# Queries asked for before keys and values, half of the first weights asked for later, and outer sums ahead of other work, at the seam of a two-part kernel

## The chip, the cores and the metric

The kernel runs on one core of one Trainium2 chip. The metric is the device time of one execution in microseconds (us), measured from outside the profile; lower is better. A profile is a separate execution, recorded by the hardware; its span, from the first to the last instruction, is a little shorter than the time of the same execution.

Engines are named as in the profile: PE is TensorE's matmuls and PEld its weight loads, DVE is VectorE, ACT ScalarE, POOL GpSimd. SP is SyncE, which here only issues DMA transfers. [...]

## The reference

Two blocks follow each other: a recurrent attention without softmax (a decaying state per head), and a feed-forward layer with a leaky ReLU.

```python
batch, n_heads, seq, head_dim = (4, 8, 768, 64)
for t in range(S):
    state = gamma[None, :, None, None] * state + np.einsum('bhd,bhe->bhde', k[:, :, t], v[:, :, t])
    y[:, :, t] = scale * np.einsum('bhd,bhde->bhe', q[:, :, t], state)
...
n_tokens, d_model, d_ff = (3072, 512, 2048)
h = x @ w_in
g = np.maximum(0.01 * h, h)
return (g @ w_out).astype(np.float32)
```

The 3072 tokens are 4 batches of 768, and the 512 columns of x are 8 heads of 64. q, k and v are float32; the weights come as float64 and are turned into float32 in the kernel.

## The kernel before, in words

**Tiles and stages.** The sequence is cut into six chunks c = 0 to 5 of 128 tokens (C = 128). A chunk of all four batches is 512 tokens, kept as two halves of N = 256. For a chunk, the attention makes x, and the feed-forward layer takes x through four units u = 0 to 3 of 512 hidden columns each. Each unit has a hidden product (x by w_in) and an output product (the activations g by w_out), added up over the units.

The attention of a chunk goes by batches b, from chunk 2 on by pairs of them. Scores are queries times keys (`scores_of_pair`, L369), sums for the state are keys times values (L380). DVE masks the scores (`am`, L387) and adds the sums to the states. Then `joint_visit` multiplies values with scores and states with queries (L444, L427) and DVE writes x (L466). POOL scales the values with the decay ahead of this (`decay_v`, L161).

Products of the feed-forward layer use seven products of half-size blocks in place of eight (Strassen's scheme in Winograd's form), with sums of blocks on DVE: `differences` makes sums of x or g, `add_sums` and `sum_of_unit` sums of weights. In the function `seven` (matmuls at L662) the products M1 to M7 of one unit are made one after another, as a generator: each step of it is one product of eight matmuls, followed by the ACT or DVE work that takes it from its PSUM bank.

**Two parts, and the seam.** In the first part (chunks 0 and 1, up to some 230 us) the float64 weights are loaded in 32 raw pieces and turned into float32 by ACT and DVE (`powers`, `begin_mantissas`, `end_mantissas`); each piece's buffer is free when DVE's instruction at L595 has read it. From the finished units more sums of weights are made and written to a DRAM buffer `kept` (`keep_unit`, L1031). In the second part (chunks 2 to 5, N2 = 16 steps n, one for each chunk and unit) the hidden product uses the scheme on two levels: `inner` (matmuls at L1182) makes seven products for each of seven outer blocks, which are split into group 0 (four blocks) and group 1 (three). `outer` adds the results of a unit up on DVE, and its leaky ReLU runs on ACT (`leaky`, L1218). The weights for `inner` are streamed from `kept`: `load_unit(n, 0)` loads `wa` (L1058, L1059) and `load_unit(n, 1)` loads `wb` (L1062, L1063). The output products stay with `seven`.

The seam is where the parts meet: the last units of chunk 1, the attention of chunk 2 and the beginning of chunk 3, and the first `inner`. What the change touches lies there.

**What sets the order.** Nothing is planned by a program: each engine gets its instructions in the order in which the code writes them. In the first part, dictionaries (`hidden_more`, `output_more`) name functions to be called after step s of a generator: `s3=[...]` means after the fourth product. In the second part the steps are drawn with `products(steps, n)`. So the order on SP is the order of calls too, and a load whose buffer is still in use holds back the loads behind it.

- When the last raw piece, n = 31, is done, `end_mantissas` asks for chunk 2's first pair: values and keys with `of_pair(2, 0, 1)` and `of_pair(2, 0, 0)` (L136), then two batches of queries and keys in another layout with `load_qk` (L119; both called queries below). These lie in buffers of the tags `qk` and `kv`, two of each, which the raw pieces 28 to 31 used before: pieces 28 and 30 those of `qk`, 29 and 31 those of `kv`.
- `begin_units` (after M1 of the output product of chunk 0, unit 3) asks for `wa` and `wb` of step 0. The buffer of `wb` is that of unit 6 of the weights, parts of which are still to be written to `kept`.
- `next_heads` (after M4 of the same product) asks for chunk 3's first pair: values, keys, then queries with `ahead`, and gives POOL the decay of the values.
- After the first part, `last`, the output product of chunk 1 and unit 3, is drawn in pieces: four products, the scores of chunk 3's first pair, M7, `inner(0, 0)`, `outer(0, 0)`, M3, `inner(0, 1)`, M4, the first product of `inner` of step 1 (`begun`), and then `outer(0, 1)`. The loop over n follows, whose first pass draws the other products of `begun`.

Of the kernel before, what the change touches and what calls it, by code (L numbers as in the profile page):

```python
# [22 lines left out]
def kernel(  # L23
# [50 lines left out]
    def new_pair(h):  # L74

        pairs = units.setdefault(N_UNITS - 1, [])
        if len(pairs) == h:
            pairs.append(work.tile([128, 2, 2, 256], FP32, tag="raw", bufs=3, name=f"last{h}"))
# [39 lines left out]
    def load_qk(c, b, queue=nc.sync):  # L118
        queue.dma_start(out=heads[c, b][0], in_=qk[c, b])  # L119
# [9 lines left out]
    def of_pair(c, b, kind, place=None):  # L129

        if place is None:
            place = work.tile([128, 2, H, D], FP32, tag="kv", bufs=AHEAD,
                              name=f"{'kv'[kind]}_{c}_{b}")
        for n in range(2):
            (keys, vals)[kind][c, b + n] = place[:, n]
        nc.sync.dma_start(out=place, in_=kv[c, b + kind])  # L136
# [69 lines left out]
    def new_o(c, name="o"):  # L206
        return work.tile([128, 4, 2, N], FP32, tag=f"o{int(c > 0)}", name=f"{name}_{c}")
# [106 lines left out]
    def ahead(c, b):  # L314

        if c >= NC:
            return
        if b < 2:
            x = work.tile([128, 2, HP, C], FP32, tag="qk", bufs=AHEAD, name=f"qk_{c}_{b}")
        else:  # L320
            if b == 2:
                room[c] = new_o(0).rearrange("p i k n -> p (i k n)")
            x = room[c][:, ds((b - 2) * 2 * HP * C, 2 * HP * C)]
            x = x.rearrange("p (s a t) -> p s a t", s=2, a=HP)
        heads[c, b] = [x]
        load_qk(c, b)
# [149 lines left out]
    def pair_of_banks(name):  # L476

        ps = two_banks(name).rearrange("p j a t -> p j (a t)")
        return [ps[:, j] for j in range(2)]
# [7 lines left out]
    def early_visit(c, b):  # L487
        def do():
            joint_visit(c, b, [pair_of_banks(f"yp{n}_{c}_{b}") for n in range(2)])
        return do  # L490
# [27 lines left out]
    def load_piece(n, place=None):  # L518
        if n >= N_PIECES:
            return  # L520
        if not f64:
            nc.sync.dma_start(out=piece(n), in_=weights[n].rearrange("p (h n) -> p h n", h=2))
            return
        if place is None:
            tag, bufs = ("raw", 3) if n < N_PIECES - 4 else (("qk", "kv")[n % 2], AHEAD)
            raws[n] = work.tile([128, W], I64, tag=tag, bufs=bufs, name=f"raw{n}")
        else:
            raws[n] = place.bitcast(I64)
        nc.sync.dma_start(out=raws[n], in_=weights[n])
# [13 lines left out]
    def end_mantissas():  # L543
        n = done["mantissas"]
        done["mantissas"] += 1
        mantissas_ended(n)
        if n != 3:
            load_piece(n + 4 if n < 3 else n + 3)
        if n == N_PIECES - 1:
            new_pair(2)  # L550
            for b in range(2):
                heads[2, b] = [work.tile([128, 2, HP, C], FP32, tag="qk", bufs=AHEAD,
                                         name=f"qk_2_{b}")]
            of_pair(2, 0, 1)
            of_pair(2, 0, 0)
            for b in range(2):
                load_qk(2, b)
        if n % 4 == 3 and n > 7:
            add_sums(n // 4)

# [37 lines left out]
    def mantissas_ended(n):  # L598
        if f64:
            z, f = zs.pop(n), piece(n)  # L600
            raws.pop(n)
            nc.vector.scalar_tensor_tensor(out=f, in0=f, scalar=2.0 ** -20, in1=z.bitcast(BF16),
                                           op0=ALU.mult, op1=ALU.mult)
# [7 lines left out]
    def add_sums(k, last=True):  # L611

        a11, a21, a12, a22, s1, s2, s4 = (block(k, i) for i in range(7))
        plus(s1, a21, a22)
        minus(s2, s1, a11)
        minus(s4, a12, s2)
        if last:
            last_sum(k)
# [194 lines left out]
    def differ(c):  # L813
        def do():
            if xs[c][1] is None:
                xs[c][1] = new_t(c, f"t_{c}")
            differences(*xs[c])
        return do
# [96 lines left out]
    steps = direct(0, 0, x, parts[0][1], 0)  # L915
# [44 lines left out]
    steps = direct(0, 0, x, parts[0][1], 1)  # L960
# [20 lines left out]
    later = hidden(1, 0, x1, t1, *parts[1][1:], order=FIRST)  # L981
# [66 lines left out]
    def at_of(n):  # L1048
        return 2 + n // NU, n % NU

    def load_unit(n, group):

        if n >= N2:
            return
        u = at_of(n)[1]
        if group == 0:
            wa = streamed[0]
            nc.sync.dma_start(out=wa[:, :, 0:1], in_=kept[u][:, :, 0:1])  # L1058
            nc.sync.dma_start(out=wa[:, :, 1:4], in_=kept[u][:, :, 3:6])  # L1059
        else:  # L1060
            wb = streamed[1]
            nc.sync.dma_start(out=wb[:, :, 0:2], in_=kept[u][:, :, 1:3])  # L1062
            nc.sync.dma_start(out=wb[:, :, 2:3], in_=kept[u][:, :, 6:7])  # L1063

    def begin_units():

        streamed.append(work.tile([128, 7, 4, C], FP32, tag="late4", name="wa"))
        load_unit(0, 0)
        flat = work.tile([128, 28 * C], FP32, tag="late6", name="wb")
        streamed.append(flat[:, 0 : 21 * C].rearrange("p (j i n) -> p j i n", j=7, i=3))  # L1070
        load_unit(0, 1)

    def next_heads():
        of_pair(3, 0, 1)
        of_pair(3, 0, 0)
        for b in range(2):
            ahead(3, b)
        for b in range(2):
            decay_v(3, b)

# [10 lines left out]
                     s3=[keep_unit(3)], s4=[early_visit(2, 2)],  # L1091
# [7 lines left out]
        (1, 2): dict(s0=[sum_of_unit(2, 3)], s1=[keep_unit(2)]),  # L1099
        (0, 3): dict(s0=[begin_units, early_scores(2, 0, spare(0))],  # L1100
                     s1=[lambda: differences(*parts[1][1:])],
                     s3=[early_visit(2, 0), differ(2), next_heads],
                     s6=[sums(2, 0)]),
    }

# [63 lines left out]
    def inner(n, group, held=False):  # L1169

        products(inner_steps(n, group, held), 8)
# [33 lines left out]
    m1, m4, m5, u2 = (made_of[0][:, :, i] for i in range(4))  # L1205
    m7, m2, m3 = (made_of[1][:, :, i] for i in range(3))

    def outer(n, group):

        if group == 0:  # L1210
            gs[n] = new_g(*at_of(n))
        g = gs[n][1]

        def to(i):
            return g[:, i].rearrange("p k (h n) -> p (k h) n", h=2)

        def leaky(i):
            nc.scalar.activation(g[:, i], g[:, i], AF.Prelu, alpha=0.01)  # L1218

        if group == 0:  # L1220
            plus(u2, u2, m1)
            plus(to(1), u2, m5)
            return
        plus(to(0), m1, m2)
        leaky(0)
        plus(to(1), to(1), m3)
        leaky(1)
        plus(u2, u2, m7)
        plus(to(3), u2, m5)
        leaky(3)  # L1230
        plus(to(2), u2, m4)
        leaky(2)

    def products(steps, n):

        for _ in range(n):
            next(steps, None)
# [22 lines left out]
    outer(0, 0)  # L1260
    products(last, 1)
    inner(0, 1)
    products(last, 1)
    begun = inner_steps(1, 0, held=True)
    products(begun, 1)
    outer(0, 1)

    for n in range(N2):
        c, u = at_of(n)
        more = n + 1 < N2  # L1270
        if u == 0:
            os[c] = new_o(c)
        visiting = c + 1 < NC and u < 2
        if n + 1 < N2:
            differences(*gs[n][1:])
        if n + 1 < N2 and u == NU - 1:
            sums_of_x(c + 1, 1)
        if n + 1 < N2:
            if n == 0:
                products(begun, 7)  # L1280
            else:
                inner(n + 1, 0, held=visiting)
            outer(n + 1, 0)
        if visiting and u == 0:
            xs[c + 1] = new_x(c + 1)
        if visiting:
            joint_visit(c + 1, 2 * u)
        steps = output(c, os[c], [gs.pop(n)], u == 0, u == NU - 1, room=room if more else last_room,
                       order=FUSED if more else LAST)
        products(steps, 3)  # L1290
        if c + 1 < NC and u < 2 and following(c + 1, 2 * u):
            scores_of_pair(*following(c + 1, 2 * u))
        if visiting:
            load_unit(n + 2, 0)
        products(steps, 1)
        if c + 1 < NC and u == 1:
            differences(*xs[c + 1])
        if c + 1 < NC and u == 2:
            sums_of_x(c + 1, 0)
        if more:  # L1300
            inner(n + 1, 1)
            for i in range(2) if visiting else ():
                ahead(c + 2, 2 * u + i)
            products(steps, 1)
            outer(n + 1, 1)
        if n + 2 == N2:
            differences(*gs[n + 1][1:])
        products(steps, 3)
# [92 lines left out]
```

## Time and profile before

| what | value |
|---|---|
| time, three runs | 642.95, 643.23, 644.82 us; median 643.23 |
| time of the profiled execution | 643.72 us |
| span of the profile | 641.8 us |
| PE busy | 632.5 us, 99% of the span |
| DVE busy | 462.5 us, 72% |
| ACT busy | 269.0 us, 42% |
| POOL busy | 22.6 us, 4% |
| bytes moved by DMA | 113.42 MB |

The page of the profile gives busy times by engine, and the span in forty slices of 16 us. Its chain of waits is followed back from the last instruction to what released each; PE has 90% of it and DMA 3%. A busy PE is not a PE at its full rate: matmuls overlap, and the clock that the chip grants PE can be lower. That clock is given in tenths for each slice. A "wait" is idle time of an engine just before an instruction, with the event that ended it. In rows of a timeline, `x32` is the number of like instructions merged into the row; names are the program's, such as `qk` for queries.

### The profile page before, as it was taken

The page shows a single profiled execution, that of the slowest core. Times are in us where ns is not written, and L with a number is a line of the kernel's source. Part 1 is how long each engine was busy: PE and PEld are TensorE (multiplying, and loading weights), DVE is VectorE, ACT ScalarE, POOL GpSimd, SP SyncE. Part 2 cuts the span into 40 slices and gives each one's busy share as a digit, 9 for nine tenths or more (in the row PEclk, how much of TensorE's full clock was granted, in tenths as well). Part 3 has the DMA queues.
Part 4 walks back from the last instruction along what each step waited for, and adds up shares of the span by engine and source line. Part 5 has one row for each costly group of instructions (what it writes and reads, how often), then busy time and mean ns, then how long its engine had stood idle before and what let it go on. Part 6 is the DMA issues. An engine that isn't in the chain of part 4 may idle for free.

```text
span 641.8 us, 14287 instructions
## 1 busy us (share of the span) xinstructions
PE 632.5 (99%) x6086; PEld 570.6 (89%) x6086; DVE 462.5 (72%) x760; ACT 269.0 (42%) x515; POOL 22.6 (4%) x45
## 2 busy tenths in 40 slices
PE   8999999999999989999999999999999999999997
PEld 5888888888888879899999998999999999999996
DVE  5679769889979956657776756778737778637655
ACT  4876557257252114352342443523424423533521
POOL 2000000000011010101000001000010000000000
PEclk9999999999999989999999999999999999999999
DMA  8931327455962988284844582854445336545201
GB/s 332 406 122 44 121 66 241 131 196 163 304 226 100 358 299 269 90 284 144 271 121 141 160 257 82 295 170 152 148 152 193 92 117 193 160 153 164 86 1 67
DMA packets 87536, 113.42 MB, mean 177 GB/s; under 512 B 3240, under 2 KB 71720, under 8 KB 87472
## 3 DMA queue, kind: packets, MB, share of 16 engines
q1 hardware_dynamic: 87168, 111.88, 52.6%
q8 instruction: 48, 0.79, 0.5%
q10 hardware_dynamic: 304, 0.62, 0.3%
q14 instruction: 16, 0.13, 0.1%
HBM read 93.35 MB, written 19.14 MB: 175 GB/s over the span
## 4 chain that ended last, share of the span: by engine, by line
PE 90%; DMA 3%; DVE 3%; ACT 1%; issue 1%; SPq 0%; DVEq 0%
PE bank L662 31%; PE bank L1182 27%; PE C_o L662 4%; PE B_o L662 4%; PE A_o L662 4%; PE A_h L662 3%; PE C_h L662 3%; PE B_h L662 3%; DMA qk<-in_qk_dram 2%; PE D_o L662 2%; PE d L683 2%; PE D_h L662 2%; PE bank L444 1%; PE bank L380 1%; PE bank L369 1%; PE bank L427 1%
## 5 line engine op out<-in xcount | busy, mean ns | idle before, releaser
L606 DVE TENSOR_TENSOR o<-o,bank 128x512 f32<-128x512 f32 (+2 forms) x91 | 58.6, 661 | 55.0 <-PE bank L662 33.5
L606 DVE TENSOR_TENSOR made<-made,bank 128x512 f32<-128x512 f32 (+1 forms) x96 | 56.4, 618 | 57.0 <-PE bank L1182 52.6
L662 PE MATMUL bank<-g,w 128*128 128x256 f32 x384 | 89.9, 382 | 0.0
L662 PEld LDWEIGHTS bank<-g,w 128*128 128x128 f32 x384 | 70.7, 190 | 9.2
L1182 PEld LDWEIGHTS bank<-x,wb 128*128 128x128 f32 x672 | 77.6, 192 | 0.8
L1182 PE MATMUL bank<-x,wb 128*128 128x128 f32 x672 | 77.6, 275 | 0.0
L1182 PE MATMUL bank<-x,wa 128*128 128x128 f32 x512 | 68.8, 276 | 0.6 <-ACT made L1188 0.6
L662 PE MATMUL bank<-gd,w 128*128 128x256 f32 x288 | 66.1, 379 | 0.0
L1182 PEld LDWEIGHTS bank<-x,wa 128*128 128x128 f32 x512 | 63.8, 192 | 2.4 <-ACT bank L1186 0.8
L662 PEld LDWEIGHTS bank<-gd,w 128*128 128x128 f32 x288 | 54.7, 190 | 7.4
L1182 PE MATMUL bank<-t,wa 128*128 128x128 f32 x384 | 53.3, 275 | 0.0
L1218 ACT ACTIVATE g<-g 128x512 f32<-128x512 f32 x64 | 39.4, 631 | 31.5 <-DVE g L606 31.5
L1182 PEld LDWEIGHTS bank<-t,wa 128*128 128x128 f32 x384 | 48.0, 192 | 0.0
L1186 ACT COPY bank<-bank 128x512 f32<-128x512 f32 (+1 forms) x32 | 16.7, 522 | 67.8 <-PE bank L1182 67.5
L606 DVE TENSOR_TENSOR g<-made 128x512 f32<-128x512 f32 x64 | 42.7, 688 | 1.1
L755 ACT COPY bank<-bank 128x512 f32<-128x512 f32 x17 | 9.7, 570 | 71.7 <-PE bank L662 71.6
L609 DVE TENSOR_TENSOR gd<-g,gd 128x512 f32<-128x512 f32 x48 | 33.2, 692 | 4.9
L773 ACT COPY bank<-bank 128x512 f32<-128x512 f32 x16 | 9.1, 570 | 49.9 <-PE bank L662 49.9
L662 PE MATMUL bank<-g,last 128*128 128x256 f32 x120 | 29.1, 388 | 0.0
L662 PE MATMUL bank<-gd,last 128*128 128x256 f32 (+1 forms) x124 | 27.5, 373 | 0.0
L662 PE MATMUL A_h<-x,w 128*128 128x256 f32 x112 | 26.6, 380 | 0.0
L662 PEld LDWEIGHTS bank<-gd,last 128*128 128x128 f32 x124 | 22.8, 190 | 3.2 <-DVE gd L609 0.3
(223 smaller groups left out, 1030.6 us busy)
## 6 DMA issues: line engine op xcount, KB each, us to landing
wa<-kept SPq DMA_DIRECT2D x16, 1344.0 KB, 7.7
raw<-in_weights_dram SPq DMA_DIRECT2D x31, 512.0 KB, 4.4
wb<-kept SPq DMA_DIRECT2D x16, 896.0 KB, 5.4
wa<-kept SPq DMA_DIRECT2D x16, 448.0 KB, 4.4
wb<-kept SPq DMA_DIRECT2D x16, 448.0 KB, 6.2
out_dram<-o SPq DMA_DIRECT2D x23, 256.0 KB, 3.4
kept<-w SPq DMA_DIRECT2D x12, 448.0 KB, 5.7
qk<-in_qk_dram SPq DMA_DIRECT2D x10, 512.0 KB, 7.9
```

The costliest lines, as they stand in the source:

```text
L369: nc.tensor.matmul(at[j][ts(h, 64), n, m, i], lhsT=x[ts(j, 64), 1, a, ts(h, 64)], rhs=x[ts(j, 64), 0, a, ts(h, 64)], start=(n == 0 and a = ...
L380: nc.tensor.matmul(sums[h][ts(j, 64), n, a], lhsT=key[ts(h, 64), 2 * a + j], rhs=val[ts(h, 64), 2 * a + j], start=(n == 0 and a == 0), sto ...
L427: mm = nc.tensor.matmul(at[n][j][ts(i, 64), m, ts(h, 64)], lhsT=by_half[h][ts(j, 64), n, a], rhs=x[ts(j, 64), 0, a, ts(h, 64)], start=(n = ...
L606: nc.vector.tensor_tensor(out=out, in0=a, in1=b, op=ALU.add)
L609: nc.vector.tensor_tensor(out=out, in0=a, in1=b, op=ALU.subtract)
L662: nc.tensor.matmul(to, lhsT=block(w, sa)[:, k, ts(i, 128)], rhs=rhs[:, k, a:z], start=(first and (i == 0 or split) and n == 0 and k == 0), ...
L683: nc.tensor.matmul(banks[r][:, i, :], lhsT=block(2 * u, r + 2 * kh)[:, k, ts(i, 128)], rhs=x[:, 2 * kh + th, k, :], start=(step == 0 and i ...
L755: nc.scalar.copy(out=bank_of("B"), in_=ps)
L773: nc.scalar.copy(out=bank_of("D"), in_=ps)
L1182: nc.tensor.matmul(ps[q][:, i], lhsT=w[:, j, i], rhs=part_of(moving[i], s), start=(i == 0 and m in ("M1", "M5", "M4")), stop=True, skip_gr ...
L1186: nc.scalar.copy(out=ps[3], in_=ps[0])
L1218: nc.scalar.activation(g[:, i], g[:, i], AF.Prelu, alpha=0.01)
```

## The change

It has three parts, and the computation stays as it was.

1. The queries are asked for ahead of values and keys, for chunk 2's first pair in `end_mantissas` and for chunk 3's in `next_heads`. Values are still asked for before keys.
2. The load of `wb` for step 0 is taken from `begin_units` and comes after `next_heads`, three products later.
3. `outer(0, 1)` is called before M4 of `last` and not after the first product of `begun`. It puts its five DVE sums into the queue at once, but collects its four leaky ReLUs in a list. Two of them come after the first product of `begun`, the other two after its third. The loop's first pass then draws five products of `begun` in place of seven.

```diff
@@ end_mantissas
+            load_qk(2, 0)
+            load_qk(2, 1)
             of_pair(2, 0, 1)
             of_pair(2, 0, 0)
-            for b in range(2):
-                load_qk(2, b)
@@ begin_units
         load_unit(0, 0)
         flat = work.tile([128, 28 * C], FP32, tag="late6", name="wb")
         streamed.append(flat[:, 0 : 21 * C].rearrange("p (j i n) -> p j i n", j=7, i=3))
-        load_unit(0, 1)
 
     def next_heads():
+        for b in range(2):
+            ahead(3, b)
         of_pair(3, 0, 1)
         of_pair(3, 0, 0)
-        for b in range(2):
-            ahead(3, b)
         for b in range(2):
             decay_v(3, b)
@@ output_more
-                     s3=[early_visit(2, 0), differ(2), next_heads],
+                     s3=[early_visit(2, 0), differ(2), next_heads, lambda: load_unit(0, 1)],
@@ outer
-    def outer(n, group):
+    def outer(n, group, later=None):
...
         def leaky(i):
+            if later is not None:
+                later.append(lambda: leaky_now(i))
+            else:
+                leaky_now(i)
+
+        def leaky_now(i):
             nc.scalar.activation(g[:, i], g[:, i], AF.Prelu, alpha=0.01)
@@ between the parts
     inner(0, 1)
+    later = []
+    outer(0, 1, later)
     products(last, 1)
     begun = inner_steps(1, 0, held=True)
-    products(begun, 1)
-    outer(0, 1)
+    for steps, leakies in ((1, later[:2]), (2, later[2:])):
+        products(begun, steps)
+        for do in leakies:
+            do()
@@ loop over n
-                products(begun, 7)
+                products(begun, 5)
```

## The prediction

> **What bounds the kernel now.** I read the page first, its busy shares and its slices, then the waits of TensorE, then the timeline where it waits, then the chain of waits there, and last the clock in chosen windows.
>
> ```profile
> PE 632.5 (99%) x6086; PEld 570.6 (89%) x6086; DVE 462.5 (72%) x760; ACT 269.0 (42%) x515; POOL 22.6 (4%) x45
> ...
> PEclk9999999999999989999999999999999999999999
> ```
>
> PE, TensorE's matmuls, is busy 99% of the 641.8 us span; VectorE (DVE) has 28% free and ScalarE (ACT) more. So an edit pays only if PE waits less, or does its work at a higher clock. One slice in forty, the fifteenth (224.6 to 240.7 us), has less than the full clock. The table of waits of PE, cut to 200 to 262 us, the seam between the two parts of the kernel, leaves four waits:
>
> ```profile
> PE bank L369 <- DMA qk<-in_qk_dram: 1.7, 2, 1.2
> ...
> PE bank L1182 <- ACT made L1188: 0.6, 1, 0.6
> ...
> PE ap L369 <- DMA qk<-in_qk_dram: 0.5, 1, 0.5
> ```
>
> After 262 us the same table is empty. The other PE waits lie in the first 34 us, which the diff does not touch. The timeline of PE at the second place (start, length, idle before in brackets):
>
> ```profile
> 229.82 1.89 PE L662 MATMUL bank<-g,last 128*128 128x256 f32 x8
> 232.86 0.69 PE L369 MATMUL bank<-qk 64*64 64x64 f32 x32 [1.15 <-DMA qk<-in_qk_dram]
> 234.13 0.69 PE L369 MATMUL bank<-qk 64*64 64x64 f32 x32 [0.57 <-DMA qk<-in_qk_dram]
> 234.64 1.96 PE L380 MATMUL bank<-v,k 64*64 64x64 f32 x64
> 236.53 2.78 PE L662 MATMUL bank<-g,last 128*128 128x256 f32 x8
> 239.15 0.38 PE L1182 MATMUL bank<-x,wa 128*128 128x128 f32 x2
> ```
>
> The scores of chunk 3 (L369) wait twice for queries. What follows without any wait is also slow: 1.96 us for 64 sums (L380), where the same 64 took 1.11 us at 210.48, and 2.78 us for eight products, where eight elsewhere take 1.89. The windows say why (length, busy times, and as the last three columns PEclk, DMA share, GB/s):
>
> ```profile
> 229.82:234.74 4.92, 3.20 (x79) 2.50 (x81) 1.38 (x2) 0.00 (x0) 2.04 (x2) 1.00 1.03 398
> 234.74:238.15 3.41, 3.41 (x76) 3.02 (x68) 2.66 (x4) 0.00 (x0) 0.00 (x0) 0.50 0.35 99
> ...
> 268.22:270.25 2.03, 2.03 (x130) 1.96 (x129) 0.81 (x2) 0.58 (x1) 0.49 (x1) 1.00 0.04 8
> ```
>
> Right after the waits the granted clock is 0.50 for 3.41 us. The third line is the same hand-over (scores and sums of a pair) with nothing to wait for: 2.03 us.
>
> [...]
>
> **Hand-over A (about 209 us): queries of chunk 2.** SP's rows:
>
> ```profile
> 185.58 0.33 SPq L136 DMA_DIRECT2D v<-in_kv_dram  x1
> 202.83 0.33 SPq L136 DMA_DIRECT2D k<-in_kv_dram  x1
> 203.21 2.34 SPq L119 DMA_DIRECT2D qk<-in_qk_dram  x2
> ```
>
> The keys take the buffer of raw piece 31, which DVE frees at 202.75 (its L595); the two query loads stand behind and land at 208.62 and 209.92. But their buffers are those of raw pieces 28 and 30, free at 181.8 and 198.96. With the edit they are issued at about 181.9 and 199.0. A lone 512 KB load takes 3.45 us to land (the values at 185.58, landed 189.03); so the second is there by about 203, 5 us ahead of need. What pays is the value load: it now passes SP behind the query load that waits until 198.96 instead of at 185.58. Issued at 199.5, it lands between 203 (3.45 us) and 205 (5.4 us, the 203.21 load behind another). POOL's two decays, 2.54 us at 202.56 now, then end at 207.6 at the latest. The keys stay at 202.83 and land by 207.4. PE wants both at 209.7 (scores at 208.69, below, and 0.99 for them), so I cost the delay at nothing. Undisturbed, the scores start at 208.69 and PE's next product at 206.77 + 1.73 (eight products) + 0.19 (change of tile shape, as at 268.22) + 2.03 = 210.72. It started at 211.52. Gain **0.80 us**. It isn't given back: the next user of ACT's copy (ends 211.97) needs it at 212.45, and the visit at 216.1 needs DVE's states, done at 213.3. The stores to `kept` also move up behind the keys, from 205.59 to about 203.2, which brings all later transfers forward.
>
> **Hand-over B (about 232 us): queries of chunk 3.** SP's order now is first weights `wa`, half weights `wb`, values, keys, queries, stores:
>
> ```profile
> 218.69 0.52 SPq L1062 DMA_DIRECT2D wb<-kept  x1
> ...
> 220.17 3.99 SPq L136 DMA_DIRECT2D v<-in_kv_dram  x1
> 224.26 0.37 SPq L136 DMA_DIRECT2D k<-in_kv_dram  x1
> 224.68 0.91 SPq L119 DMA_DIRECT2D qk<-in_qk_dram  x2
> ```
>
> The DMA engines are full from 206 to 235 us (share 1.03, 398 GB/s in the window above), so a transfer lands when the bytes ahead of it are through: `wb` 229.04, v 230.32, k 231.59, queries 232.82 and 234.09, some 1.26 us per 512 KB. `wb` isn't read before 247. After the edit the queries follow `wa` (landed 224.84 now): even if nothing were earlier they land at 226.1 and 227.4, the values at 228.7, keys 229.9, `wb` at about 234.1, the same bytes in another order. Their buffers are free when PE has read chunk 2's queries (217.3). PE wants the queries at 230.9 (231.74 − 0.80), and values at 231.9; POOL's decay, 2.04 us, ends at 230.7. No wait is left, and with no idle time I expect no half-clock window. Undisturbed: 229.82 + 1.73 + 0.19 = 231.74 for the scores, + 2.03 = 233.77, + 1.83 (270.25 to 272.08) = 235.60 for the first inner product; it was 239.15. Gain **3.55 us**: 1.12 and 0.78 of waiting, 1.65 of half clock (3.41 × 0.5 would be 1.7). Bounds: 1.90, if the clock dips all the same, and 3.55. `wb` at 234 is wanted at 247.13 − 4.35 = 242.8: hidden. The stores and loads behind `wb` on SP wait with it; their readers come at 268.
>
> **Hand-over C (about 259 us): outer sums and copies.** No instruction is added; 5 DVE sums (0.69 us each) pass one DVE addition, and two of four leaky ACTs pass behind two copies. ACT now:
>
> ```profile
> 255.12 1.18 ACT L1218 ACTIVATE g<-g 128x512 f32<-128x512 f32 x2
> 257.00 1.23 ACT L1218 ACTIVATE g<-g 128x512 f32<-128x512 f32 x2 [0.70 <-DVE g L606]
> 258.14 0.57 ACT L1188 COPY made<-bank 128x512 f32<-128x512 f32 x1
> ```
>
> The copy of M5 stands behind four leakies that wait for DVE, so PE stalls for it, and M7 then waits for M6's copy. After, in the clock of before: DVE's sums run 253.04 to 256.2 (they fill the 0.71 us in which DVE waits now); ACT copies M1 to 255.2, leakies to 256.3, M5 to 256.8, M4 to 257.3, leakies to 258.4, M6 to 258.9. PE wants M5's copy at 258.0 and M6's at 258.9. Undisturbed, PE would do 7 × 0.893 from 253.54 and begin the visit at 259.89; it did at 260.82, 0.93 later. I take 0.06 for M6 and get **0.87 us**, bounds 0 and 0.93. The DVE addition and its store come 2.4 us later; that tile is overwritten at 266.6, after the store has landed (260.85 now, about 262). DVE's differences end near 260.0 as now; the reader of the first is PE at 263.8.
>
> **Sum.** 0.80 + 3.55 + 0.87 = 5.22 us. From 262 us on PE is the bound, and loads are triggered by PE, so the gain stays. Span 641.8 − 5.2 = 636.6. That run took 643.72 us; the median of the others is 643.23 (642.95 to 644.82), so the time is **638.0**.
>
> **Rivals.** (1) The half clock comes back although the waits are gone, from the small matmuls of the seam. Against it: the same matmuls at 268 and 296 ran at 1.00. 5.22 − 1.65 = 3.57: 639.7. (2) A new wait eats A and C: the values, decayed late, at A, and M6's copy or DVE at C. For it: DVE has no pause from 204.2 to 213.5. It gives 3.55: 639.7. (3) The order isn't what holds the queries, but buffers not yet free; the two query waits stay and only C works: 642.4. Against it: the L595 ends above. (4) The slower side: `wb`, now last on SP, lands too late for the first group-1 product. Each us after 242.8 costs one; from 248.0 the gain is gone, from 249.9 it is measurably slower. That is 14 us later than the full engines need for the same bytes, and I see only a wait of SP for a buffer that could do it.
>
> **How the numbers follow.** Mine 0.75, (1) 0.10, (2) 0.08, (3) 0.04, (4) 0.03. Less than 0.3% (1.9 us) can't be told from no change here. Faster: mine, (1) and (2), 0.93; the same: (3); slower: (4). My case alone is 637.0 to 638.9 (C's bounds, and the spread of the runs before). The range reaches to (1) and (2) with that spread (0.3 below the median, 1.6 above, of which I take 0.6): 636.8 to 640.3.
>
> **What would show it.** Right: no wait of PE for queries near 209 and 231 us, PEclk at 9 in all middle slices, the scores at L369 taking 2.03 us with the sums, no wait for L1188 near 254, and the stage after 262 as long as before. Wrong: a wait for `wb` or for POOL's values, or a half-clock window elsewhere.

## The result, and the profile after

The changed kernel takes 639.01 us (median of four runs, 638.92 to 639.29); the kernel before took 643.09 beside it (four runs, 642.79 to 644.82). The ratio is 0.9932, with a 95% interval of 0.9914 to 0.995: faster by 4.1 us. (Here and below the ratio compares all runs, so it differs a little from that of the medians.) The forecast was 638.0 with a range of 636.8 to 640.3. The profile's span went from 641.8 to 637.2 us. The first lines of its page, as for the kernel before (busy time and share of each engine; clock in 40 slices):

```profile
PE 630.4 (99%) x6086; PEld 569.1 (89%) x6086; DVE 462.3 (73%) x760; ACT 269.0 (42%) x515; POOL 22.6 (4%) x45
...
PEclk9999999999999999999999999999999999999999
```

PE does the same 6086 matmuls, and the slice with the low clock is gone. The table of PE's waits, from 34 us to the end, has one line left (total, times, longest, in us):

```profile
PE bank L427 <- DVE made L606: 0.2, 1, 0.2
```

The line is new: a wait of matmuls of the joint visit for DVE. The waits for queries and for ACT's copy (L1188 before, L1187 in the changed kernel, whose lines have shifted) are gone. Hand-over B in PE's timeline (start, length), to be read against the six rows of before:

```profile
228.93 1.89 PE L662 MATMUL bank<-g,last 128*128 128x256 f32 x8
230.75 1.16 PE L369 MATMUL bank<-qk 64*64 64x64 f32 x64
231.73 1.25 PE L380 MATMUL bank<-v,k 64*64 64x64 f32 x64
232.91 1.99 PE L662 MATMUL bank<-g,last 128*128 128x256 f32 x8
234.74 0.38 PE L1181 MATMUL bank<-x,wa 128*128 128x128 f32 x2
```

The scores are one group of 64 with no bracket behind them, and the first inner product starts 5.81 us after the product at 228.93; before it took 9.33 (229.82 to 239.15). The windows of the same length as the half-clock one (columns: PE, PEld, DVE, ACT, POOL busy, then clock, DMA share, GB/s):

```profile
231.33:234.74 3.41, 3.41 (x112) 3.14 (x105) 2.79 (x5) 0.00 (x0) 0.00 (x0) 1.00 0.91 290
234.74:238.15 3.41, 3.41 (x32) 3.41 (x31) 2.54 (x5) 2.26 (x4) 0.00 (x0) 1.00 0.61 177
```

The clock is 1.00 in both. SP's order at B, as it was issued:

```profile
217.00 1.42 SPq L119 DMA_DIRECT2D qk<-in_qk_dram  x2
218.47 0.48 SPq L136 DMA_DIRECT2D v<-in_kv_dram  x1
219.07 0.41 SPq L136 DMA_DIRECT2D k<-in_kv_dram  x1
219.57 0.61 SPq L1062 DMA_DIRECT2D wb<-kept  x1
220.23 4.13 SPq L1063 DMA_DIRECT2D wb<-kept  x1
```

When the starts of PE's groups are set side by side, before against after, the 4.6 us come about as 0.86 at hand-over A, 3.52 at B and 0.22 at C; the rest, 0.03, is from the first 34 us. These figures say where PE gained time in these two profiles, not what each part of the change is worth by itself; the experiments below look at that. After C the difference stays at 4.63 to 4.65 us up to the end.

### The profile page after: what moved, and what is told of

The parts are those of the page before. It is cut to its first block, busy times and chain, and to the rows that moved or that the text cites. A ratio compares the mean times of both kernels' runs of the same rounds, so it can differ in the third digit from the quotient of the medians.

```text
span 637.2 us, 14289 instructions
## 1 busy us (share of the span) xinstructions
PE 630.4 (99%) x6086; PEld 569.1 (89%) x6086; DVE 462.3 (73%) x760; ACT 269.0 (42%) x515; POOL 22.6 (4%) x45
## 4 chain that ended last, share of the span: by engine, by line
PE 95%; DVE 2%; ACT 1%; DMA 1%; issue 0%; DVEq 0%; ACTq 0%
PE bank L662 32%; PE bank L1181 27%; PE C_h L662 4%; PE B_o L662 4%; PE A_h L662 4%; PE C_o L662 4%; PE A_o L662 4%; PE B_h L662 4%; PE D_h L662 2%; PE D_o L662 2%; PE d L683 2%; PE bank L369 1%; PE bank L444 1%; PE bank L427 1%; PE bank L380 1%; DMA t<-decay_dram 1%
```

## Experiments

The first four split the change. Numbers in brackets behind a time are the lowest and highest run, those behind a ratio its 95% interval. One window of 3.41 us at half clock takes 0.0027 off the mean clock of a run of 641.8 us (half of 3.41, divided by 641.8; the profiled run of before, which has one, shows 0.997), so a mean clock of 0.997 or less is taken as the sign of one; only the profiled run of each kernel shows where it lay.

**Chunk 2's queries alone (a_only).**

```diff
+            load_qk(2, 0)
+            load_qk(2, 1)
             of_pair(2, 0, 1)
             of_pair(2, 0, 0)
-            for b in range(2):
-                load_qk(2, b)
```

> Only chunk 2's queries ahead of its values and keys; chunk 3's loads, wb and the outer sums as before. Theory 1 (the DMA stream from 203 us on is full, and its end is set by its bytes): hand-over A gains 0.85 us as in the changed kernel, but chunk 3's queries are still last in the stream and land near 234 us as before, so PE waits at hand-over B for what it gained at A, and the half-clock window stays: span 641.6 to 641.9, time 643. Theory 2 (the stores to kept start 2.4 us earlier, and all later loads with them): the queries land near 232 us, the waits at B shrink to under 1 us and the clock stays full: span 638.5 to 639.5. Theory 3 (each hand-over for itself): span 641.0.

Measured: 640.74 us (639.34 to 644.47), ratio 0.9954 (0.9937 to 0.9971), span of the profiled run 641.2. Its PE rows at B, and the clock window after the wait:

```profile
228.72 1.89 PE L662 MATMUL bank<-g,last 128*128 128x256 f32 x8
232.65 0.69 PE L369 MATMUL bank<-qk 64*64 64x64 f32 x32 [2.03 <-DMA qk<-in_qk_dram]
233.89 1.13 PE L369 MATMUL bank<-qk 64*64 64x64 f32 x32 [0.55 <-DMA qk<-in_qk_dram]
...
233.35:236.77 3.42, 2.88 (x97) 2.77 (x97) 1.29 (x2) 0.00 (x0) 0.00 (x0) 0.50 0.13 49
```

In the profiled run it goes as theory 1 has it: PE arrives 1.1 us earlier, and its first wait grows from 1.15 to 2.03 us. The queries, still last in the stream, landed at 232.60 and 233.84 (232.82 and 234.09 before), although the values and keys ahead of them landed 1.0 us earlier than before (229.34 and 230.58). Of the 1.1 us 0.6 were left at the first inner product (238.52, before 239.15). But this run is one of the six with a low mean clock (0.996). In the other 14 it was 0.999 or more, and the median of their spans is 638.7, against 640.65 in the like runs of before: 1.95 us, more than A's 0.86. Theory 2, a stream that comes earlier, would explain that, but no trace of such a run was kept, so it stays open.

**Chunk 3's part alone (b_only).**

```diff
-        load_unit(0, 1)
...
     def next_heads():
+        for b in range(2):
+            ahead(3, b)
         of_pair(3, 0, 1)
         of_pair(3, 0, 0)
-        for b in range(2):
-            ahead(3, b)
...
-                     s3=[early_visit(2, 0), differ(2), next_heads],
+                     s3=[early_visit(2, 0), differ(2), next_heads, lambda: load_unit(0, 1)],
```

> Only chunk 3's part: its queries ahead of values and keys, and wb after them; chunk 2's queries and the outer sums as before. Theory 1 (order at B is what counts): the wait at 210 us stays (0.8 us), the waits at 233 us and the half-clock window go, gain 3.5 us: span 638.3, time 639.6. Theory 2 (B's gain needs the earlier stores of part A): the queries or the decayed values come late, PE waits again after 231 us: span 640 or more.

Measured: 640.91 us (640.24 to 642.92), ratio 0.9957 (0.9938 to 0.9976), span 638.8. PE's waits after 34 us:

```profile
PE ap L369 <- DMA qk<-in_qk_dram: 1.2, 1, 1.2
PE bank L1181 <- DMA wa<-kept: 0.4, 1, 0.4
```

Theory 1 holds: hand-over B gained 3.52 us, as in the whole change, though the wait at A was 0.6 us longer in this run than in the profile of before. There is a new one, 0.4 us for step 1's first weights `wa`, which turns up again below. B's gain needs nothing from A.

**The half weights back in front (wb_first).**

```diff
         load_unit(0, 0)
...
+        load_unit(0, 1)
...
-                     s3=[early_visit(2, 0), differ(2), next_heads, lambda: load_unit(0, 1)],
+                     s3=[early_visit(2, 0), differ(2), next_heads],
```

> The changed kernel with wb put back ahead of chunk 3's loads. Theory 1 (the move of wb is what gets the values in time): chunk 3's queries land at 229.5 to 231 us, the values near 232, POOL has them decayed near 234, and PE waits some 2.4 us at L380 from 231.7 us, perhaps with a half-clock window after it: span 639.5 to 641.3. Theory 2 (queries first is enough, wb is hidden anyway): span 637.2 as in the changed kernel.

Measured: 640.01 us (638.91 to 644.51), ratio 0.9952 (0.9937 to 0.9968), span of the profiled run 637.2. My 2.4 us were wrong for that run: PE has no wait at B in it. POOL's row and PE's row for the sums:

```profile
230.11 2.04 POOL L161 TENSOR_TENSOR v<-v,dec 128x512 f32<-128x512 f32 x2 [12.51 <-DVE o L606]
...
231.90 1.25 PE L380 MATMUL bank<-v,k 64*64 64x64 f32 x64
```

The values landed at 229.95, not near 232: the stream was further ahead (`wa` landed at 222.06 there, at 224.33 in the changed kernel's profile). POOL starts 0.16 us after that, as in the changed kernel (228.17 and 228.33); the bracket names an instruction of DVE that ended in between. It finishes at 232.15, inside PE's group of sums that uses its result, so there is no room to spare. But this run is the fastest of the 20. They spread over 5.6 us, three with a mean clock of 0.997 or less. The ten runs of the changed kernel in two sets lie within 638.58 and 639.29; 18 of the 20 here are slower than all of them, and the median is higher by 1.0 to 1.2 us. So the move of `wb` buys nothing in the best runs and about 1 us in the median. That late values are what the slower runs wait for is argued; none of them was traced.

**Outer sums and copies alone (c_only).**

```diff
...
+    later = []
+    outer(0, 1, later)
     products(last, 1)
     begun = inner_steps(1, 0, held=True)
-    products(begun, 1)
-    outer(0, 1)
+    for steps, leakies in ((1, later[:2]), (2, later[2:])):
+        products(begun, steps)
+        for do in leakies:
+            do()
...
-                products(begun, 7)
+                products(begun, 5)
```

> Only the outer sums and leaky ReLUs moved; all loads as before. The prediction's figure: gain 0.87 us, span 640.9. What the trace of the changed kernel shows: 0.63 us gained until the visit begins and 0.36 us given back there, since PE's reads wait for DVE's M3 addition to leave bank 1; gain 0.2 to 0.3 us, span 641.5, time 642.8.

Measured: 643.86 us (641.62 to 645.59), ratio 1.0012 (0.9999 to 1.0024), span of the profiled run 640.4. Group by group, PE gained 0.63 us until the visit and gave back 0.41 there, as in the whole change. The time shows nothing, as 0.22 us would not. The profiled run has no half-clock window although PE still waited for queries at B (0.74 and 0.73 us; 1.15 and 0.57 in the profile of before), as the windows show:

```profile
231.00:234.50 3.50, 2.03 (x42) 1.39 (x41) 1.05 (x2) 0.00 (x0) 1.75 (x2) 1.00 1.03 396
234.50:238.00 3.50, 3.50 (x105) 3.23 (x106) 2.57 (x4) 0.00 (x0) 0.00 (x0) 1.00 0.67 185
```

So waiting doesn't always bring the window; the fillers below take this up.

The three hand-overs can also be compared by the runs with a mean clock of 0.999 or more. Their median spans are 640.65 before, 638.7 with A's edit alone, 638.8 with B's, 640.6 with C's, and 637.1 in the ten runs of the whole change. So A's edit alone is worth about as much as B's alone, which the 0.86 and 3.52 us read from the two profiles don't show. Why is open, as said at a_only.

**The changed kernel again, and three edits of hand-over C.** These were run together with the kernel before on one chip.

> The changed kernel as it is, to have it on the same chip as the next three. Span 637.2 us and time 639.0 in all runs, within 0.3 us, and full clock in all of them, since no wait of PE is left that could start a half-clock window.

Measured: 638.77 us (638.58 to 639.09), ratio 0.9923 (0.9897 to 0.9949), span 637.3, the clock full in all six runs. In the changed kernel the rows of DVE and PE at C are:

```profile
252.47 0.68 DVE L609 TENSOR_TENSOR gd<-g 128x512 f32<-128x512 f32 x1
253.68 1.49 DVE L609 TENSOR_TENSOR gd<-g,gd 128x512 f32<-128x512 f32 x2 [0.52 <-ACT g L1223]
255.09 0.68 DVE L609 TENSOR_TENSOR g<-g 128x512 f32<-128x512 f32 x1
255.69 1.88 DVE L606 TENSOR_TENSOR made<-made,bank 128x512 f32<-128x512 f32 x3
...
255.78 0.46 PE L444 MATMUL bank<-am,v 64*64 64x64 f32 x16
256.42 0.69 PE L427 MATMUL bank<-qk,states 64*64 64x64 f32 x32 [0.18 <-DVE made L606]
```

These rows are the beginning of the visit (`joint_visit`). PE's reads of the states (L427) write to bank 1 of PSUM (`bank[1]` in the kernel), and before that DVE's addition of M3 (the first of the three at 255.69) must have read the product M3 out of this bank: it ends near 256.4, and PE's reads start at 256.42. The addition stands behind four differences, and the second of these waits 0.52 us for the third leaky ReLU on ACT.

*leaky_early:* the third leaky ReLU ahead of M5's copy, the fourth ahead of M4's.

```diff
-    for steps, leakies in ((1, later[:2]), (2, later[2:])):
+    for steps, leakies in ((1, later[:3]), (1, later[3:]), (1, [])):
```

> The changed kernel with the third leaky ReLU ahead of M5's copy and the fourth ahead of M4's, in place of both behind M4's. Theory 1 (DVE's differences wait for the late leaky ReLUs and hold up its M3 addition, which PE's reads need): DVE ends its differences 0.6 us earlier, M6's copy is 0.3 us earlier, both waits of PE go: gain 0.5 us, span 636.7. Theory 2 (DVE is bound by its own work there): only M7's wait goes, gain 0.1 to 0.2 us, span 637.05.

*diff_late:* the last difference behind the three additions.

```diff
-            differences(*gs[n][1:])
+            differences(*gs[n][1:], last=n > 0)
...
                 products(begun, 5)
+                last_difference(gs[n][1])
```

> The changed kernel with the last of the four differences of step 0 behind DVE's three additions of inner(1, 0), not ahead of them. Theory 1 (PE's reads wait for bank 1, which DVE's M3 addition leaves): that addition comes 0.6 us earlier and the wait of 0.18 us at L427 goes: gain 0.35 us, span 636.85. Theory 2 (the reads wait for something else, the values' matmuls or POOL's memset): no gain, 637.2.

*both:*

> Both of these edits. No more can be had than PE's undisturbed pace, so 0.5 us, span 636.7, as leaky_early if theory 1 holds there; if not there, then here.

Measured: leaky_early 638.63 us (638.33 to 638.95), ratio 0.9922 (0.9898 to 0.9945), span 637.0; diff_late 638.40 (638.28 to 639.25), ratio 0.992 (0.9897 to 0.9944), span 636.9; both 638.27 (638.17 to 638.81), ratio 0.9918 (0.9895 to 0.9942), span 637.0. In all three the wait at L427 is gone, and the traces show 0.41 us won there. The rows of diff_late, with no bracket:

```profile
255.22 2.09 DVE L606 TENSOR_TENSOR made<-made,bank 128x512 f32<-128x512 f32 x3
...
256.19 0.65 PE L427 MATMUL bank<-qk,states 64*64 64x64 f32 x32
```

So either way of bringing DVE's addition forward is enough, and theory 1 holds for both edits. In the profiles of the first two, nearly as much was lost to a wait of 0.37 and 0.35 us for step 1's weights, near 249.7 us; it is the one of b_only, and the profiles of the changed kernel and of both don't have it. The line of leaky_early:

```profile
PE bank L1181 <- DMA wa<-kept: 0.4, 1, 0.4
```

**A better version (best).** Both edits, and chunk 3's second pair of queries asked for behind `inner(0, 0)` and its weight load.

```diff
     scores_of_pair(3, 0)
-    for b in range(2):
-        ahead(3, 2 + b)
     products(last, 1)
     sums_of_x(2, 1)
     inner(0, 0)
+    for b in range(2):
+        ahead(3, 2 + b)
```

> The changed kernel with both edits at hand-over C (leaky ReLUs earlier, last difference later) and the loads of chunk 3's second pair of queries behind the first inner product and its weight load. Two of the last profiles showed PE waiting 0.35 us for step 1's first weights near 249.7 us, behind those queries in the stream. If the order on the queue is the cause, that wait goes in every run: span 636.4 to 636.6, time 638.1. If the stream is short of bandwidth anyway, or the queries come late for 263 us, no gain over both: 638.3 or more.

Measured: 638.13 us (638.02 to 638.49), ratio 0.9915 (0.9898 to 0.9931), span of the profiled run 636.8, the other four 636.3 to 636.4. Step 1's weights landed at 248.49, ahead of the product that starts near 249, and from 34 us on PE has no wait in the profile. Against the changed kernel PE gains 0.29 us until the visit and 0.41 in it; with C's 0.22 that makes 0.92, all but 0.01 of the 0.93 us that PE lost at C before. It is the fastest version here. Against the changed kernel it is worth about 0.6 us, one part in a thousand, which the traces show group by group, while the intervals of the two ratios overlap. Against both (638.27) the difference is within their spread, and since the profile of both has no wait for step 1's weights either, it isn't shown that the new place of the query loads is what keeps that wait away.

**Fillers in the kernel before (fill8, fill16).** Does waiting start the half-clock window?

```diff
+    for _ in range(8):
+        fill(6)
     scores_of_pair(3, 0)
```

> The kernel before, with eight filler matmuls (512 columns, 0.216 us each, into a PSUM bank that is overwritten later) ahead of chunk 3's scores, so that PE works for 1.73 us where it waited for the queries. Theory 1 (idle time of PE starts the half-clock window): scores begin at about 233.5 us as late as before, but the clock stays at 1.00 after them, in nearly all runs: where the profile of before has the window, this one is 1.6 us shorter, span 640.2, and the share of runs with a mean clock of 0.997 or less, 25 of 61 before, falls to a tenth or less. Theory 2 (the small matmuls, or the load as such, start it): the share stays near 4 in 10, and the span 641.8.

Measured: 643.26 us (642.41 to 647.36), ratio 1.0006 (0.9991 to 1.0021), span 642.6; 3 of 14 runs had a mean clock of 0.997 or less, 6 of 22 of before beside them. This was inconclusive: in its profile the queries came at 235.16 and 236.43 only, later than before, and PE waited 1.25 and 0.56 us behind the fillers. The clock stayed at 1.00 in this profile (the run's mean is 1.000, and the 64 sums behind the waits took 1.17 us, 1.96 in the profile of before), although these 1.81 us are more than the 1.72 us that the half clock followed in the profile of before.

> As fill8, with sixteen filler matmuls (3.46 us), since with eight the queries landed only at 235.2 and 236.4 us and PE still sat idle for 1.81 us behind the fillers. PE now works until about 235.2 us, so that little or no idle time is left at hand-over B, although the scores begin later than they could. Theory 1 (idle time of PE starts the half-clock window[...]): hardly any run has a mean clock of 0.997 or less; one in ten may, from the wait at 210 us, as in the run of chunk 3's part alone (1 of 10). Before: 25 of 61 and 6 of 22. Span near 641.7 us with the full clock. Theory 2 (matmuls, load or chance of the seam whatever PE waits): the share stays at 3 to 4 in 10.

Measured: 644.30 us (642.91 to 646.08), ratio 1.0012 (1.0001 to 1.0022), span of the profiled run 641.9. None of the 22 runs had a low clock; 11 of 27 of before beside them did. The rows of PE, with no bracket:

```profile
229.93 1.89 PE L662 MATMUL bank<-g,last 128*128 128x256 f32 x8
231.65 3.62 PE L695 MATMUL bank<-mask 128*128 128x512 bf16 x16
235.20 1.16 PE L369 MATMUL bank<-qk 64*64 64x64 f32 x64
236.18 1.25 PE L380 MATMUL bank<-v,k 64*64 64x64 f32 x64
237.36 2.00 PE L662 MATMUL bank<-g,last 128*128 128x256 f32 x8
```

Scores that start 2.3 us later than in the profile of before are followed by a first inner product only 0.04 us later (239.19 and 239.15). The seam's matmuls and loads are those of before, and a wait at A is still there (1.06 us here, 0.52 in the profile of before); the idle time at B is gone, and the window with it. The fillers also move the scores to 235.20 us, where less may be left of the stream (in the profile of before the DMA share is 0.35 from 234.74 to 238.15 us), but in the changed kernel the scores ran beside the stream (a DMA share of 0.91 from 231.33 to 234.74 us) and no run had a low clock. So theory 1 holds: the window at B needs the idle time there. What decides in which runs it comes is not shown. The fillers are no gain, for with 3.46 us they last longer than the waits that they fill (1.72 us in the profile of before).

**The half weights later still (wb_late).** In the changed kernel the load of `wb` is put behind chunk 3's second pair of queries.

```diff
-                     s3=[early_visit(2, 0), differ(2), next_heads, lambda: load_unit(0, 1)],
+                     s3=[early_visit(2, 0), differ(2), next_heads],
...
     for b in range(2):
         ahead(3, 2 + b)
+    load_unit(0, 1)
     products(last, 1)
```

> The changed kernel with the load of wb put later still, behind chunk 3's second pair of queries. It would be issued near 237.6 us and land near 246; the first product of group 1 wants it at 242.7. Rival 4 of the prediction as a mechanism (each us after that costs one): PE waits 3 to 3.6 us, perhaps with a half-clock window of 1.7 us after it: span 640.5 to 642.5. If wb were hidden there too: 637.2.

Measured: 640.79 us (640.19 to 641.57), ratio 0.9959 (0.9942 to 0.9975), span 639.1. PE's waits:

```profile
PE bank L1181 <- DMA wb<-kept: 1.6, 2, 1.1
PE bank L427 <- DVE made L606: 0.2, 1, 0.2
```

The mechanism of rival 4 is real, with a smaller size than I wrote: the two loads of `wb` landed at 243.66 and 244.96, a good us earlier than expected. PE waits 1.07 us for the first, with which group 1's products begin (at 242.72 in the changed kernel), and 0.53 us for the second. The span is 1.9 us longer than the changed kernel's. In the changed kernel `wb` landed at 233.95, nearly 9 us ahead of need.

## Why the prediction was right, and where it was off

**Bound and gain by waits.** Right. PE's work is the same, all of the gain is idle time and clock, and what PE won at the seam it kept to the end. The time measured, 639.01, is in the range, but just above the 637.0 to 638.9 that the prediction gave for its own case: it fell inside because the range reaches to rivals (1) and (2), of which only a part of (2) came true.

**Hand-over A: 0.80 forecast, 0.86 measured.** The queries were issued at 181.84 and 199.00 (forecast 181.9 and 199.0). The values landed at 203.7 and POOL ended their decay at 206.6 (forecast 207.6 at the latest), the keys landed at 207.30 (207.4). So the delay of the values cost nothing, as claimed.

**Hand-over B: 3.55 forecast, 3.52 measured.** The full stream was the right model: "the same bytes in another order" gave 227.4, 228.7, 229.9 and 234.1 for queries, values, keys and `wb`; they landed at 226.89, 228.17, 229.47 and 233.95. POOL's decay ended at 230.4 (230.7). No half-clock window came. That it would go with the waits was an assumption of the forecast; the profile of before has one such place, where 1.72 us of idle time, in two waits, went ahead of 3.41 us at 0.50. fill16 bears it out: with PE's idle time there filled, none of 22 runs had a low clock, and 11 of 27 of before beside them did.

**Hand-over C: 0.87 forecast, 0.22 measured.** This step failed. My times for ACT and DVE were near: M6's copy was to end at 254.5 and DVE's differences near 255.6 (less the 4.4 us by which all is earlier there); they ended at 254.65 and 255.77. In the profile of before ACT started the copy of M5 at 258.14, behind four leaky ReLUs, though its product had ended near 255.4: what held the copy was read rightly. But I asked who reads the differences, and not what is queued behind them on DVE. The addition of M3 was, and PE's reads need the bank that it empties; the sum of 0.87 has nothing for it. Before the change PE came there late enough:

```profile
260.28 1.93 DVE L606 TENSOR_TENSOR made<-made,bank 128x512 f32<-128x512 f32 x3
...
261.10 0.65 PE L427 MATMUL bank<-qk,states 64*64 64x64 f32 x32
```

In the changed kernel 0.41 us were given back at that wait, and 0.29 ahead of the visit in place of 0.06: M7, which needs M6's copy, starts 0.19 us late (254.69), and the rest is lost within it. diff_late and leaky_early confirm the first, and best wins back both amounts. Why the copies were late I can only argue: M5's copy started at 252.05, 0.2 us later than ACT was free, just after DVE's last outer sum (251.95), which reads the tile that the copy writes. This wait wasn't tried by itself.

**From span to time: 638.0 forecast, 639.01 measured.** C explains 0.65 us of the difference. The rest is in the step "so the time is": I took the whole difference of the spans from a median. The profile of before had the half-clock window, but only 46 of 121 runs of before in the four later sets had a mean clock of 0.997 or less. In the first of these sets (61 runs) the median span is 642.8 us in the runs with a low mean clock and 640.65 in the others; in the ten runs of the changed kernel it is 637.1. So the change is worth some 3.5 us against the runs without the window and 5.7 against those with it. The median that I started from is a mix of both, 0.49 us below the 643.72 of the run whose profile I read; from that run, the 4.6 us measured lead to 639.1.

**The rivals.** (1), a half clock for other reasons, falls: no run of the changed kernel has a low clock, and fill16 shows that the seam's matmuls do not bring it. (2), a new wait in place of A and C, came true at C alone. (3) falls: the order on SP was what held the queries, which at A went out at 203.21 behind the keys (202.83, just after DVE's read at L595 ended at 202.75), and at 181.84 and 199.00 when they stood ahead of them. (4) is a true mechanism, but 9 us away.

## What to carry to other kernels

When a bound engine waits for a transfer in a full stream, count the bytes ahead of it and reorder by who needs what first: nothing gets faster, but the first consumer stops waiting (PE's 1.72 us at B are gone), and a load with 18 us to spare (`wb` before: landed at 229.04, read from 247.13) goes last. When a wait of TensorE goes, look whether a low clock came behind it (0.50 for 3.41 us here), and over many runs, since one profile shows only one draw. When work is put ahead in an engine's queue, list everything queued behind it and what each of these frees, down to the PSUM bank (here DVE's addition of M3 behind four differences, for which PE waited 0.18 us).

## What was not expected of the hardware

- 1.72 us of idle time of PE, in two waits, was followed by 3.41 us at half clock in the profile of before, and one wait of 2.03 us by 3.42 us in a_only's. The amount alone doesn't decide: 1.81 us in two waits in fill8's profile, 1.6 us in wb_late's and 1.47 us in c_only's were followed by no such window. By the mean clock it came in 46 of 121 runs of the kernel before, in none of 22 with the idle time at B filled, and in none of the 33 runs of the changed kernel, leaky_early, diff_late, both and best; with a wait left at A (b_only) in 1 of 10, and in wb_first in 3 of 20.
- The stream's pace varies from run to run: the larger load of `wa`, 1344 KB, landed 9.8 to 11.8 us after its issue in the profiles of the changed kernel, leaky_early, diff_late and both, whose transfers are the same up to there. The version with no room to spare at hand-over B in its profile (wb_first) has a wide spread (638.91 to 644.51), the changed kernel a narrow one (638.58 to 639.29); that the first comes from the pace is argued.
